# Attention, mixture of heads and a gated feed-forward on one core: four plain float32 pairs in batch 0 in place of two, under a new order table

## The chip, the cores and the metric

The kernel runs on one core of one Trainium2 chip. Its five engines run their own queues in order and wait for one another through semaphores: TensorE (PE) multiplies matrices into the eight PSUM banks, VectorE (DVE), ScalarE (ACT) and GpSimd (POOL) do elementwise work (POOL on SBUF alone in this kernel), and SyncE (SP) issues the transfers. The metric is the device time of one execution in microseconds (us); less is better.

## The reference

Three stages follow one another, all in float32, for 4 batches of 448 positions:

```python
# attention: q, k, v are [4, 12, 448, 64]
scores = scale * q @ k.T;  causal mask;  attn = softmax(scores);  x = attn @ v   # heads joined: [4, 448, 768]
# mixture: a gate picks 2 of 4 heads per position (weights from the gate's softmax over the two)
for e in range(4):
    a = softmax(causal(scale * (x @ wq[e]) @ (x @ wk[e]).T))
    out += gate[e] * (a @ (x @ wv[e]) @ wo[e])
# feed-forward: w_in is [768, 1024], a 3-tap convolution along the sequence gates the hidden values
h = relu(out @ w_in);  y = (h * sigmoid(conv3(h))) @ w_out
```

## The kernel before

A pair is two heads of one batch: `A0_3` is pair 3 of batch 0 of the attention (6 pairs a batch, 24 in all), `M1_0` a pair of the mixture (2 a batch). The second last number of a tile's name is the pair, a last `_1` or `_0` the head.

For each pair the steps are these. `prep` loads q and k. The *split form* loads each head onto both halves of the partitions (`nat`), copies it as float32r (the high part, line 333, 331 or 337) and subtracts to get the low part (line 340: one piece of 128x448 for k, one of 64x448 for q); on the stacked tile `sk` a head then needs two matmuls per row block (line 637). The *plain form* (`j.plain`) loads the pair once and `pair_scores` multiplies in plain float32 with 64 rows per head, both heads in turn for each row block (line 595); PE runs each such matmul as two records. The row blocks are 448, 336, 224 and 112 wide, since the mask is causal. DVE takes mask and row maximum out of PSUM into `P` (line 650), ACT the exponential (659), DVE the sum and reciprocal (667, 670), then POOL, ACT or DVE normalise the rows (333, 331, 337), PE transposes them against the identity (690, ten 112x112 blocks a head), ACT or DVE evacuate into `PT`, and PE multiplies with v in plain float32 (760, 16 records a pair, named PV here). Scores use the PSUM banks 0, 1 and 4 in turn (`s` in `BANKS`), transposes 2, 3 and 5, products 4 and 5.

Out of a batch's six `xT` tiles PE projects q, k (952) and v with the gate (998) of the mixture's heads, whose pairs then go the same way. The weights wo and w_in are folded into one matrix on the way (881, with conversions on DVE, ACT and POOL, lines 417 to 434, 869, 872), the feed-forward's first product is line 1188, its gate lines 1201 to 1226, and the output product line 1251 with 576 matmuls.

The order of all this isn't the program's: every step is a task, and a table (`ORDER`, decoded by `steps_of`) lists task numbers with the engine that runs each. `Program.run` goes through it, takes banks and buffers as the tasks ask for them, and issues each task's instructions there. So the table sets each engine's queue, and for steps that two or three engines can do, which of them does it. Where its own plan sees PE idle, it fills in matmuls of the identity (`warm`, line 1320), into a bank that `idle_bank` finds.

Of the kernel before, what the change touches and what calls it, by code (L numbers as in the profile page):

```python
# [1384 lines left out]
```

## Time and profile before

| | us |
|---|---|
| three runs | 500.73, 504.17, 504.58 (median 504.17) |
| profiled execution, its own time | 503.03 |
| its span, first to last instruction | 501.2 |
| PE busy in the span | 487.5 |
| DVE busy | 369.0 |
| ACT busy | 349.8 |
| POOL busy | 261.9 |

The span is what the trace shows of the execution; the 1.8 us around it are no instruction's. A busy PE counts the time in which a matmul is under way, and records of neighbouring matmuls overlap, so how much work PE has done is counted from the number of matmuls and the time that one takes in an unbroken stretch.

### The profile page before, as it was taken

How to read it: one execution, taken by the hardware profiler on the slowest of the kernel's cores; microseconds unless marked ns; L12 is line 12 of the kernel's file. 1: busy time of each engine (PE TensorE's matmuls, PEld its weight loads, DVE VectorE, ACT ScalarE, POOL GpSimd, SP SyncE). 2: the span in 40 equal slices, each digit the busy share in tenths (PEclk: the TensorE clock that was granted, in tenths of full speed). 3: DMA queues.
4: the chain of work that ended last, by engine and by line, in shares of the span. 5: the costliest groups of instructions: out<-in, count | busy, mean ns of one | idle time of the engine just before them, and what ended most of it. 6: DMA issues, size and time to landing. Idle time of an engine off the chain costs nothing.

```text
span 501.2 us, 9905 instructions
## 1 busy us (share of the span) xinstructions
PE 487.5 (97%) x3202; PEld 419.7 (84%) x3202; DVE 369.0 (74%) x1110; ACT 349.8 (70%) x970; POOL 261.9 (52%) x388
## 2 busy tenths in 40 slices
PE   8788999999999999999999999999999999999997
PEld 6656878988888898888988788898999989999996
DVE  4999999988899686987789984487587556374300
ACT  5989999998889768886888893386566554344201
POOL 1856879978879777998788944162022002000000
PEclk9999999999999999999999999999999999999999
DMA  8857468996793767665688615838220112101011
GB/s 216 211 164 186 128 179 225 232 250 192 203 242 106 178 173 214 142 176 136 202 204 237 151 57 168 272 148 213 88 90 0 56 37 80 51 16 58 37 38 73
DMA packets 29171, 73.03 MB, mean 146 GB/s; under 512 B 4160, under 2 KB 11072, under 8 KB 28352
## 3 DMA queue, kind: packets, MB, share of 16 engines
q1 hardware_dynamic: 29040, 72.18, 51.8%
q8 instruction: 25, 0.41, 0.4%
q10 hardware_dynamic: 80, 0.23, 0.2%
q14 instruction: 26, 0.21, 0.1%
HBM read 50.50 MB, written 13.63 MB: 128 GB/s over the span
## 4 chain that ended last, share of the span: by engine, by line
PE 74%; DVE 11%; POOL 5%; DMA 4%; issue 2%; ACT 1%; SPq 0%; POOLq 0%; DVEq 0%; ACTq 0%
PE bank L1251 23%; PE bank L952 9%; PE bank L690 9%; PE bank L760 9%; PE bank L637 9%; PE bank L1188 8%; PE bank L998 4%; DMA nat<-in_qk_dram 4%; DVE P_A L650 3%; PE bank L881 3%; POOL sk_A L340 2%; DVE PT_A L337 1%; POOL P_M L333 1%; POOL P_A L333 1%; DMA cwraw<-in_conv_w_dram 1%
## 5 line engine op out<-in xcount | busy, mean ns | idle before, releaser
L1251 PE MATMUL bank<-g,wout 128*128 128x448 f32 x576 | 123.2, 367 | 0.0
L1251 PEld LDWEIGHTS bank<-g,wout 128*128 128x128 f32 x576 | 107.4, 188 | 8.8
L659 ACT ACTIVATE P_A<-P_A,nm_A 112x448 f32<-112x448 f32 (+3 forms) x192 | 99.4, 521 | 15.7 <-DVE nm_A L650 10.4
L340 POOL TENSOR_TENSOR sk_A<-nat,sk_A 64x448 fp32r<-64x448 f32 (+1 forms) x77 | 90.3, 1172 | 9.7 <-ACT sk_A L331 3.9
L650 DVE CUSTOM_DVE_ANT_0 P_A<-bank,mask 112x448 f32<-112x448 f32 (+3 forms) x192 | 80.0, 440 | 10.8 <-PE bank L595 6.3
L637 PE MATMUL bank<-sk_A 128*112 128x112 f32 (+3 forms) x352 | 66.4, 312 | 3.5 <-DVE nm_A L650 2.9
L952 PE MATMUL bank<-xT,wqk 128*128 128x448 f32 x288 | 68.7, 374 | 0.6 <-DVE sk_M L968 0.4
L690 PE MATMUL bank<-ident,P_A 112*112 112x112 f32 x480 | 61.7, 264 | 3.3 <-DVE xT L792 1.4
L333 POOL TENSOR_SCALAR P_A<-P_A,r_A 112x336 f32<-112x336 f32 (+3 forms) x97 | 49.9, 526 | 25.7 <-DVE r_A L670 9.2
L637 PEld LDWEIGHTS bank<-sk_A 128*112 128x112 f32 x352 | 48.8, 176 | 10.1 <-DVE nm_A L650 4.5
L690 PEld LDWEIGHTS bank<-ident,P_A 112*112 112x112 f32 x480 | 49.8, 135 | 8.0 <-DVE xT L792 1.6
L952 PEld LDWEIGHTS bank<-xT,wqk 128*128 128x128 f32 x288 | 51.2, 188 | 4.1 <-DVE sk_M L968 0.5
L1209 DVE SCALAR_TENSOR_TENSOR bank<-h,cw,bank 128x448 f32<-128x448 f32 x64 | 43.5, 687 | 14.8 <-ACT bank L1207 11.6
L760 PE MATMUL bank<-PT_A,v 112*64 112x448 f32 (+3 forms) x384 | 50.4, 406 | 0.1
L760 PEld LDWEIGHTS bank<-PT_A,v 112*64 112x64 f32 x384 | 26.2, 137 | 23.6 <-issue 12.3
L331 ACT ACTIVATE P_A<-P_A,r_A 112x448 f32<-112x448 f32 (+3 forms) x87 | 42.3, 517 | 4.6 <-DVE r_A L670 4.3
L1188 PE MATMUL bank<-ocs,wp 128*128 128x448 f32 x192 | 43.5, 367 | 0.0
L998 PE MATMUL bank<-wvg,xT 128*112 128x260 f32 x288 | 41.2, 287 | 0.2 <-DVE wm L434 0.2
L333 POOL TENSOR_SCALAR sk_A<-nat 128x896 fp32r<-128x896 f32 x35 | 33.0, 941 | 12.6 <-DMA nat<-in_qk_dram 11.6
L1188 PEld LDWEIGHTS bank<-ocs,wp 128*128 128x128 f32 x192 | 35.7, 188 | 3.0
L659 ACT ACTIVATE P_M<-P_M,nm_M 112x224 f32<-112x224 f32 (+3 forms) x64 | 33.3, 522 | 6.8 <-DVE nm_M L650 5.3
L331 ACT ACTIVATE PT_A<-bank 112x336 f32<-112x336 f32 (+1 forms) x75 | 33.9, 472 | 5.2 <-PE bank L690 5.0
(105 smaller groups left out, 820.2 us busy)
## 6 DMA issues: line engine op xcount, KB each, us to landing
nat<-in_qk_dram SPq DMA_DIRECT2D x88, 224.0 KB, 4.0
wraw<-in_w_in_dram SPq DMA_DIRECT2D x12, 512.0 KB, 5.5
woraw<-in_w_out_dram SPq DMA_DIRECT2D x12, 512.0 KB, 5.1
wo<-wohl SPq DMA_DIRECT2D x12, 512.0 KB, 4.1
wout<-wo SPq DMA_DIRECT2D x6, 1024.0 KB, 10.0
v<-in_v_dram SPq DMA_DIRECT2D x24, 224.0 KB, 4.5
out_dram<-osb SPq DMA_DIRECT2D x24, 224.0 KB, 1.9
sk_M<-sk_M SPq DMA_DIRECT2D x16, 224.0 KB, 4.2
```

Of the source, the lines that this page charges most:

```text
L331: nc.scalar.activation(dst, src, AF.Copy, scale=scale)
L333: nc.gpsimd.tensor_scalar(dst, src, scale, 1.0 if scale2 is None else scale2, ALU.mult, ALU.mult)
L340: (nc.gpsimd if e == "POOL" else nc.vector).tensor_tensor(dst, a, b, op)
L637: nc.tensor.matmul(sp[:CP], t[:, j.o[h], m * CP : (m + 1) * CP], t[:, j.o[h] + k, :w], start=(k == 2), stop=(k == 1),)
L650: nc.vector.tensor_tensor_reduce(rows(i), st["s", i][:CP, :w], mask[:, S - w :], -SCALE, 3.0e38, ALU.add, ALU.min, st["nm"][:, i : i + 1],)
L659: nc.scalar.activation(rows(i), rows(i), AF.Exp, bias=st["nm"][:, i : i + 1], scale=-1.0, accum_out=st["sm"][:, i, 0:1],)
L690: nc.tensor.transpose(pt[:CP, o : o + CP], rows(i)[:, kt * CP : (kt + 1) * CP], ident[:CP, :CP])
L760: nc.tensor.matmul(st["ov"][h * D : (h + 1) * D, kt * CP : S], j.v[:, kt, h, :], j.PT[h][:, col_base[kt] : col_base[kt] + S - kt * CP], st ...
L952: nc.tensor.matmul(st["ps"][:, :S], proj["wqk"][:, a, cc, w, p * P : (p + 1) * P], xT[b, cc][:, b2, :], start=(cc == 0 and (a, b2) == PASS ...
L998: nc.tensor.matmul(st[i][:CP, :VW], xT[b, cc][:, a, i * CP : (i + 1) * CP], proj["wvg"][:, b2, cc, :], start=(cc == 0 and (a, b2) == PASSE ...
L1188: nc.tensor.matmul(st["ps", c][:, :S], wp[:, a, ec, c * P : (c + 1) * P], st["oc", ec][:, b2], start=(ec == 0 and (a, b2) == PASSES[0]), s ...
L1251: nc.tensor.matmul(st["ps"][:, :S], ffn["wout", n][:, a, c], gs[c][:, b2], start=(c == 0 and (a, b2) == PASSES[0]), stop=(c == NFC - 1 and ...
```

## The change

Pairs 2 and 3 of batch 0 take the plain form, as pairs 0 and 1 do already; their loads, scores and what feeds these change with it. The order table is another. A condition in `idle_bank` is added that holds for all eight banks.

```diff
-    "c-jrtxmQ{VqX2NYpm5n_6WQSc;$;!JfXb$<Dx0#(I)#`i#F;`(3N>FLW(qa)&WU8+IcTOZWC}G?s7aw_ieRQtGesm*sF^~|6fR#8%@i(Ey!TK1"
...
+    "c-jTQNj#eg!vOH)NkUdho+Pr0?6U7<Cwa0j$SRBPfX)H!fwTwoJ)m<yzk}!;&^d_C!SWu^9!TE<`X10Zh|U2s2eb!t4x)2F`~803|BpwqkS9nx"
...
                 o = self.owner.get(k)
-                if o is None or (o.left == 0 and o.ready <= since):
+                if k < 8 and (o is None or (o.left == 0 and o.ready <= since)):
                     return k
...
     for j in order:
-        j.plain = j.kind == "A" and j.b == 0 and j.p < 2
+        j.plain = j.kind == "A" and j.b == 0 and j.p < 4
```

What the table moves is seen in the queues themselves. Lines of the changed kernel are one lower (594 is 595 of before). On PE, just behind the plain scores of pair 1, this stood (`sk1_A0_2` is head 1 of pair 2 in split form, bank 2, 3 and 5 hold transposes):

```order
L637 MATMUL bank0_61<-sk1_A0_2_192 112x448 x2
L637 MATMUL bank4_65<-sk1_A0_2_192 112x224 x2
L637 MATMUL bank4_65<-sk1_A0_2_192 112x112 x2
L690 MATMUL bank2_63<-ident_71,P_A0_0_0_150 112x112 x4
L690 MATMUL bank3_64<-ident_71,P_A0_0_0_150 112x112 x3
L1320 MATMUL bank5_66<-ident_71 128x128 x2
L637 MATMUL bank1_62<-sk1_A0_2_192 112x336 x2
L690 MATMUL bank5_66<-ident_71,P_A0_0_0_150 112x112 x3
```

and this stands there now, with pair 2's plain scores of both heads on `sk0_A0_2`:

```order
L594 MATMUL bank1_62<-sk0_A0_2_217 112x448
L594 MATMUL bank4_65<-sk0_A0_2_217 112x448
L1319 MATMUL bank2_63<-ident_71 128x128 x2
L594 MATMUL bank0_61<-sk0_A0_2_217 112x336
L594 MATMUL bank1_62<-sk0_A0_2_217 112x336
L689 MATMUL bank2_63<-ident_71,P_A0_1_1_186 112x112 x4
L689 MATMUL bank3_64<-ident_71,P_A0_1_1_186 112x112 x3
L689 MATMUL bank5_66<-ident_71,P_A0_1_1_186 112x112 x3
L594 MATMUL bank0_61<-sk0_A0_2_217 112x224
L594 MATMUL bank1_62<-sk0_A0_2_217 112x224
```

The split scores of one head are replaced by plain ones of both heads, and the row blocks have transposes of pair 1 between them.

On POOL the queue began, behind the setting up of the masks, with the split parts of pairs 2 and 3 (`sk` from `nat`) and one normalisation of `P` a head:

```order
L333 TENSOR_SCALAR sk1_A0_2_192<-nat_0_2_1_193 128x2x448
L333 TENSOR_SCALAR P_A0_0_1_146<-P_A0_0_1_146,r_A0_0_1_148 112x336
L340 TENSOR_TENSOR sk1_A0_2_192<-nat_0_2_1_193,sk1_A0_2_192 128x448
L340 TENSOR_TENSOR sk1_A0_2_192<-nat_0_2_1_193,sk1_A0_2_192 64x448
L333 TENSOR_SCALAR P_A0_0_0_150<-P_A0_0_0_150,r_A0_0_0_152 112x336
L340 TENSOR_TENSOR sk1_A0_3_271<-nat_0_3_1_272,sk1_A0_3_271 128x448
L340 TENSOR_TENSOR sk1_A0_3_271<-nat_0_3_1_272,sk1_A0_3_271 64x448
L333 TENSOR_SCALAR P_A0_1_1_207<-P_A0_1_1_207,r_A0_1_1_209 112x448
```

and begins now with normalisations alone, up to the first split pair, which is pair 4:

```order
L332 TENSOR_SCALAR P_A0_0_1_146<-P_A0_0_1_146,r_A0_0_1_148 112x448
L332 TENSOR_SCALAR P_A0_0_1_146<-P_A0_0_1_146,r_A0_0_1_148 112x224
L332 TENSOR_SCALAR P_A0_0_0_150<-P_A0_0_0_150,r_A0_0_0_152 112x448
L332 TENSOR_SCALAR P_A0_0_0_150<-P_A0_0_0_150,r_A0_0_0_152 112x336
L332 TENSOR_SCALAR P_A0_0_0_150<-P_A0_0_0_150,r_A0_0_0_152 112x112
L332 TENSOR_SCALAR P_A0_0_0_150<-P_A0_0_0_150,r_A0_0_0_152 112x224
L332 TENSOR_SCALAR P_A0_1_1_186<-P_A0_1_1_186,r_A0_1_1_188 112x336
L332 TENSOR_SCALAR P_A0_1_1_186<-P_A0_1_1_186,r_A0_1_1_188 112x224
L332 TENSOR_SCALAR P_A0_1_0_190<-P_A0_1_0_190,r_A0_1_0_192 112x336
L332 TENSOR_SCALAR P_A0_1_0_190<-P_A0_1_0_190,r_A0_1_0_192 112x448
L332 TENSOR_SCALAR sk1_A0_4_335<-nat_0_4_1_336 128x2x448
L339 TENSOR_TENSOR sk1_A0_4_335<-nat_0_4_1_336,sk1_A0_4_335 128x448
```

Eight steps on `sk` before pair 1's last normalisation have gone, and POOL does two to four normalisations of a head where it did one.

On DVE, where the evacuations of pair 1 (`PT_A0_1`) are half done, this stood:

```order
L337 TENSOR_SCALAR PT_A0_1_1_1_339<-bank2_63 112x336
L337 TENSOR_SCALAR P_A0_1_0_211<-P_A0_1_0_211,r_A0_1_0_213 112x224
L340 TENSOR_TENSOR sk0_A0_3_386<-nat_0_3_0_387,sk0_A0_3_386 128x448
L650 ISA P_A0_2_0_377,nm_A0_2_0_378<-bank1_62,mask_76 112x336
L650 ISA nm_A0_2_0_378 112x1
L667 TENSOR_REDUCE r_A0_2_1_257<-sm0_88 112x4
L337 TENSOR_SCALAR PT_A0_1_1_0_340<-bank3_64 112x448
L670 RECIPROCAL r_A0_2_1_257<-r_A0_2_1_257 112x4
L650 ISA P_A0_2_0_377,nm_A0_2_0_378<-bank0_61,mask_76 112x112
```

and this stands there now (row maxima of pair 3 come in):

```order
L666 TENSOR_REDUCE r_A0_2_0_293<-sm1_90 112x4
L336 TENSOR_SCALAR PT_A0_1_1_0_309<-bank2_63 112x336
L649 ISA P_A0_3_1_391,nm_A0_3_1_392<-bank0_61,mask_76 112x448
L649 ISA nm_A0_3_1_392 112x1
L669 RECIPROCAL r_A0_2_0_293<-r_A0_2_0_293 112x4
L649 ISA P_A0_3_0_395,nm_A0_3_0_396<-bank4_65,mask_76 112x336
L649 ISA nm_A0_3_0_396 112x1
L649 ISA P_A0_3_1_391,nm_A0_3_1_392<-bank1_62,mask_76 112x336
```

The slow normalisation on line 337 and the low part on line 340 have left the stretch, and row maxima of the pair behind have moved up.

## Rows read from the trace of the kernel before

**Rows 1.** The page's first part: busy us (share) and instructions of each engine.

```profile
PE 487.5 (97%) x3202; PEld 419.7 (84%) x3202; DVE 369.0 (74%) x1110; ACT 349.8 (70%) x970; POOL 261.9 (52%) x388
```

**Rows 2.** Stretches: length, busy (x count) of PE, PEld, DVE, ACT, POOL, clock, DMA.

```profile
17.00:34.00 17.00, 13.37 (x91) 10.50 (x90) 16.62 (x52) 14.94 (x48) 11.97 (x13) 0.90 0.71 191
34.00:51.00 17.00, 14.79 (x110) 10.90 (x109) 16.90 (x51) 15.78 (x50) 9.58 (x11) 1.00 0.65 175
51.00:68.00 17.00, 16.57 (x121) 13.04 (x120) 16.79 (x60) 16.44 (x54) 15.42 (x20) 1.00 0.56 142
```

**Rows 3.** Waits of PE from 75 us on: us in total, times, longest.

```profile
PE bank L637 <- DVE nm_A L650: 0.4, 1, 0.4
...
PE bank L998 <- DVE wm L434: 0.2, 1, 0.2
```

**Rows 4.** PE's groups up to 73.6 us: count, busy us, mean ns, idle before.

```profile
L637 PE MATMUL bank<-sk_A 128*112 128x448 f32 (+3 forms) x97 | 18.8, 321 | 3.4 <-DVE nm_A L650 2.9 <-DVE xT L792 0.3
L690 PE MATMUL bank<-ident,P_A 112*112 112x112 f32 x130 | 17.6, 274 | 2.9 <-DVE xT L792 1.4 <-DVE P_A L337 0.7 <-DVE PT_A L337 0.4
L760 PE MATMUL bank<-PT_A,v 112*64 112x448 f32 (+3 forms) x96 | 13.0, 411 | 0.0
...
L952 PE MATMUL bank<-xT,wqk 128*128 128x448 f32 x30 | 7.8, 383 | 0.0
L595 PE MATMUL bank<-sk_A 64*112 64x448 f32 (+3 forms) x32 | 7.4, 444 | 0.7 <-DVE nm_A L650 0.7
```

**Rows 5.** The chain in order of time: start us, us, what.

```profile
68.31 1.23 PE bank L952 x6
69.54 1.11 PE bank L637 x8
70.65 0.96 PE bank L690 x10
71.61 2.04 PE bank L760 x16
...
461.70 35.88 PE bank L1251 x177
```

**Rows 6.** Plain scores: first block's stretch (length, PE, PEld); timeline's last (start, us).

```profile
5.49:6.52 1.03, 1.03 (x4) 0.36 (x4) 1.00 0.99 386
...
15.21 0.76 PE L595 MATMUL bank<-sk_A 64*112 64x112 f32 x4 [0.44 <-DVE nm_A L650]
```

**Rows 7.** Groups by shape over the span: count, busy us, mean ns, idle before.

```profile
L340 POOL TENSOR_TENSOR sk_A<-nat,sk_A 64x448 fp32r<-64x448 f32 x42 | 50.0, 1191 | 5.4 <-ACT sk_A L331 1.4 <-POOL P_A L333 0.8
L337 DVE TENSOR_SCALAR PT_A<-bank 112x336 f32<-112x336 f32 x44 | 21.5, 497 | 0.1
L331 ACT ACTIVATE PT_A<-bank 112x336 f32<-112x336 f32 x52 | 22.7, 443 | 3.9 <-PE bank L690 3.9
L331 ACT ACTIVATE P_A<-P_A,r_A 112x448 f32<-112x448 f32 x23 | 15.1, 661 | 1.9 <-DVE r_A L670 1.9
L331 ACT ACTIVATE sk_A<-nat 128x896 fp32r<-128x896 f32 x9 | 8.5, 948 | 0.5 <-DMA nat<-in_qk_dram 0.5
L340 DVE TENSOR_TENSOR sk_A<-nat,sk_A 128x448 fp32r<-128x448 f32 x9 | 7.7, 851 | 0.7 <-ACT sk_A L331 0.7
L337 DVE TENSOR_SCALAR P_A<-P_A,r_A 112x224 f32<-112x224 f32 x3 | 2.5, 833 | 0.0
L340 DVE TENSOR_TENSOR sk_A<-nat,sk_A 64x448 fp32r<-64x448 f32 x2 | 1.2, 622 | 0.1
```

**Rows 8.** Waits up to 75 us, longest first: us in total, times, longest.

```profile
POOL sk_A L333 <- DMA nat<-in_qk_dram: 11.0, 3, 9.8
```

**Rows 9.** PE's timeline from 20.93 us, and one stretch (columns as in rows 2).

```profile
20.93 0.57 PE L637 MATMUL bank<-sk_A 128*112 128x336 f32 x2 [1.95 <-DVE nm_A L650]
...
23.01 2.09 PE L690 MATMUL bank<-ident,P_A 112*112 112x112 f32 x10
...
20.00:30.00 10.00, 8.83 (x53) 6.55 (x53) 10.00 (x35) 9.59 (x32) 7.66 (x9) 0.83 0.66 174
```

More of the change, by code (lines that the diff above doesn't have):

```diff
@@ new lines @@
+    "t|LpxZRAkZ2I?Gji5jb#s5(HFktI|Gb%*MP!K-?!3RSaJROIi3L&9%pOclFISVgLmR)tV8RIzHgYOgAX>O%FS22k?qV0E<mgrKj^R(Dn3S6@}%"
+    "RO_pts$f;TDqHow>TQ*^8iO7|DX|8u4Qr|DtNuc`Bvc4cH50vE1w$WIT~ysxxv`@tK5P>8gYYW~Rx?mNT#cz2t)8qdRKKoXt$th0LzB=8)t6Np"
+    "=t0a7MuxtxDx;69j?p@_4edrJ&|!25J%%|)PhilnQuR)C1e?HiVt3IM^c}i@nZ+Dbm#e8YjGEKx^XdaM98<*P(B0@fb{IQ_<<~4>)-ji8G=_{B"
+    "#rC5I&|4TL#*E=%3Rs{TQ$2znLmy*iv3r<B>=t$zyNx}>tYIHv<+vP9ha*=H;<|AVE{IcL3>XL#$Mj(SjTTi;p_Mh-njbg>9)~C6A-tu=Qxm9("
+    ")dcbT*c`qa&%q1vGJF8Djk&<&YI<tQ*eI?SbBUQoXD~Ya9Qqb>j{&fG{4jnJFN1x?{)v6S%Ly)mj?jx6!kKYnxEt&x_6ZhA#Zk%B{+cKrjh)0j"
@@ new lines @@
+    "V6ixmz@)+nqxfmO7S@Yr;dnSRVF?!?fLI2WNtnaKaYg(#o`ib>8-|6bBh(l*LoHDG*fsoX+#B30+y-tJcZ55}^-%LQztLCeZ|Pg~Yx*8;6W>SO"
+    "#Enr|j0#=H7=um1&;%YKM#vHdV5@k5aezO?U*pg4ck~JBEEU5bF)na?MgdmAi>L~!foh`yGz^VJE92*D7Hjmhr-a9Z=Y&Uual#B?k+4#;QS)E="
+    "9=%K-pcbji)F915yTZ*8__Rqv1@|X?k+IB}g-ID})DP4p!XEXAal&xY-cygL7t|{%iDqWF7*bk^5oGKzt{72Tmex(P<2MLfgdM^yb)@EhMXyA!"
+    "MQ=n$B0zjhU1RJqZWz6cGsZmw&O8w@#Y40^>L0XY+IY=GO()|q?GYov$TP+n6AX;FP{U)sgKffw7(1|QQAKnonqkZ__F<)(-I~3ca?MlP3)&QI"
+    "p0+~!O#4b>)#_`@uuv_(HdfnR`v$fGv(%ErXQBn#8jZo6rcszUrkrVIhL|2|iS`5bZ_!)Pd(j8cl(;08)}Fx5U|(UkFrL_13xoI8exXxq|Dk=S"
@@ new lines @@
+    "A!;+VQKpWGfxDPwI1?@t^Wjps0X|qeT&oki#XGcu_*d_;cb~TIUGV0ZUChziXUrkyqSy)#h<C(W-evKQch8HfJ*vH~?PH$Qmc`dKw>1wn01=>L"
+    "iB5Q>HVFT#=8N|ircJyij*9ohv*PL6oVZ_{gm;Mt#3N#m$RIN574N+lL+2C6#Ft(k{jBz`_675k_a(E$yk_n&kC-P+xUa&L6ZOPn@wxa)jPbp!"
+    "eO+rMLPQc>Mt{v*tlg;n%ez&(TN@(oF-g9?+Bh*ogtL}vyNPd@tIRxWn5CnSvKCqW#5{3?h?9I5BP8F%phO_qVr{cxbha-*&%nFkeegl}FkC7b"
+    "Cr%NkSbE7B(=54T&JgE_w<I^+M$gf|)Ogs-tRQ<7{t~`I+#vSTOT=Abfpt$pvx-DAi^+<yJJ|=sBjP!cA-N)+5Z^I>g)hKGzBSe?tBbx2AEA%Z"
+    "4J-j!M&4(^$OH5h@+rAOo`J8!%d9Q<pDZcs8}W{)B_l{SmXKv3JIUwd9rzyn6I|)D__V$$y31Ff&(U!t3W-e;lJ3ZttlveDBp|_(Z&*LEd)ZIf"
@@ new lines @@
+    ">tu)(XZ5f$tTR?GE5O<%2YoS#jAS6id>P*<{DB2yW7#Y=iOpkE>z?_@WCnSkJmfnh+ej`_m=q(8`6hi+>=L`cF0+r>o8(1y!MDs_W6${(e3#@P"
+    "IYv&_J!e1i$=MJm&k1sN*ip_fr-#%}%9C;&cAc=UlhjFugOi+T&MbR`G){U%-eY6Hr{u@v5%Lsilru^ugWa5Swyds~GfkQ!U9n-DJN6WLp1eTL"
+    ")#dA^>WX#4b)$6!a-nXvZjrP?+8~ukyQBk>v97yr)i=kn148f%yvTXtyM*`FE!F+ZR)9LTg}q+4RcEVXgL)7G<KQ9bgcJbHpt}yo3D<$#Z)}kB"
+    "KazL8F3EPCfa3(D90upOE(`X6z2FDVTh10|m2<#3<eYLU@OwCu3kNU&2{`9K+$=Z9z2@9-^c)LE&J6-OZj}46?hEO$q>KBh?xOCt?!NA-?x}<g"
+    "!~lSc=JL2^ZXb7$`-=OVJIbBlj({_u02l)&z!h)@oCCAK0=N!tf_vb<BoCZ<?gF<P=mlO#CMB;VW$*<241NW_f#1QuNqWi(R|;4tAxeyrp{#Rz"
@@ L93 @@
+    "u0NO0P32~Cq0af-Vs0h3kt^kfb3f;HbNjhJa`DbwXHREu=d;fL2eqS|O#"
 )
```

104 lines of the change are left out of this document (41 added, 63 removed).

## The prediction

> **What bounds the kernel now.** I read the engine totals first, then stretches of the span, then who waited for whom, then the chain that ended last. TensorE (PE) is busy for 97% of the span, VectorE (DVE) for 74%, ScalarE (ACT) for 70%, GpSimd (POOL) for 52% [rows 1]. These are averages over two regimes, and the stretches tell them apart. From 17 to 68 us PE is busy for 44.7 of 51 us, while DVE is busy for 16.62 + 16.90 + 16.79 = 50.3 and ACT for 14.94 + 15.78 + 16.44 = 47.2 [rows 2]. After 75 us the waits put down to PE are five, of 0.4, 0.4, 0.3, 0.2 and 0.2 us, 1.5 us in all (first and last in [rows 3]). So there is a head of some 70 us in which softmax, evacuation and weight work on DVE and ACT feeds PE, and a body in which PE runs its queue without stopping. The chain says the same: from about 68 us it is PE nearly everywhere, and it ends with 35.88 us of output products in one piece [rows 5].
>
> What the head costs can be counted. When PE ends the weighted values of the last pair of batch 0 (A0_5), at 71.61 + 2.04 = 73.65 us [rows 5], it has done the work of [rows 4]: 96 score matmuls (12 heads; the row has one more that starts at the edge), 130 transposes, 96 records of PV, 30 projection matmuls and 2 plain pairs. At the rates of unbroken stretches [rows 5] that is 12 x 1.11 + 13 x 0.96 + 6 x 2.04 + 5 x 1.23, and 2 x 2.6 for the plain pairs (below): 13.3 + 12.5 + 12.2 + 6.2 + 5.2 = 49.4 us. PE has lost 24.3 us by then. That is what a change to batch 0 can win from.
>
> **The change part by part.** The sum is made against the profiled execution's own 503.0 us (span 501.2 us and 1.8 us around it). The median of the three runs is 504.2, so 1.1 above it, and one run was at 500.7.
>
> *PE work.* Pairs A0_2 and A0_3 lose four split heads, 4 x 1.11 = 4.4 us [rows 5], and get two plain pairs. The 448-wide row block of a plain pair, both heads, took 1.03 us in the first, undisturbed place [rows 6]; scaled by columns (1120 over 448) a pair is an estimate of 2.6 us, so two are 5.2. Below, the bound is no change: 40% of the columns of two split heads are worth 0.89 us at 1.11 a head, not far from 1.03. Above it is the busy time of the plain scores' records, waits between paired records included, 7.4 us for two pairs [rows 4], or +1.5 a pair. I take the estimate: **+0.8 us** (0 to +3.0).
>
> A plain score makes two PE records, which is 2 for a head's block where the split form also has 2 [rows 4, 6]. The Trainium skill, page "FP8 and Floating Point Precision", section "TensorE Precision Notes", says that true float32 takes four passes through the array. By that rule a plain pair would cost twice the split one, 2 x 2.2 us, so the sum would be 3.6 us higher, 504.2 us, still within 1% and for 0.04 of the chance of (c) below; the 1.03 us of the row speaks for a price near that of two.
>
> *PE order.* Up to the end of A0_5's products the new order holds 64 split score matmuls, 127 transposes, 24 projection matmuls, as many PV products and 4 plain pairs: 8.9 + 12.2 + 4.9 + 12.2 + 10.4 = 48.6 us. That is 0.8 less than the 49.4 above, and must be done later: **+0.8 us**.
>
> *DVE.* Up to the last evacuation before those products (PT_A0_5) the new order takes off DVE three normalisations of 112x224 (3 x 0.833), five evacuations of 336 (5 x 0.497) and one of 448 (0.6), three low parts 128x448 (3 x 0.851), and about 0.9 us of smaller things; it adds four low parts 64x448 (4 x 0.622) [rows 7]. That is 2.5 + 2.5 + 0.6 + 2.6 + 0.9 - 2.5 = 6.6 us of records; records on DVE overlap their successors by some 0.07 us and there are 11 fewer, so 5.8 us of time.
>
> *ACT.* To the same point: four normalisations of 448 fewer (4 x 0.661) and three smaller ones (about 0.4 each), two high parts fewer (2 x 0.948), one small exponential fewer (0.6), five evacuations of 336 more (5 x 0.443) and one of 448 (0.5), one weight copy more (0.6) [rows 7]: 2.6 + 1.2 + 1.9 + 0.6 - 2.2 - 0.5 - 0.6 = 3.0, with overlaps 2.7 us.
>
> *POOL* sheds eight low parts of 64x448 (8 x 1.191 = 9.5 us) [rows 7] and takes over ten normalisations, so its queue gets no longer while one of these takes under 0.95 us. It had room in the head (11.97 of 17 us from 17 to 34) [rows 2], so this is priced at nothing; the cover is that room, and were it gone, the normalisations that moved to POOL would make transposes late.
>
> *DMA and SP.* The plain loads carry each pair once where the split form carries it twice, 448 KB less a pair. POOL waited 9.8 us for the first split load [rows 8], but DVE had the row maxima of two pairs to do meanwhile, so nothing is counted. On SP the load of A0_1 moves ahead of the convolution weights, whose small steps on DVE and ACT come later; A0_2's load follows, and is needed only when two pairs' row maxima are read. The `k < 8` holds for every bank and changes nothing. After batch 0 the table changes banks and interleaving, with equal counts per kind on PE, so nothing is counted; the bounds are -1.5 us (the waits of [rows 3] gone) and +2 us (as much again and a little more).
>
> *How much of the relief reaches PE.* Between 17 and 68 us DVE idled 0.7 us and ACT 3.8 [rows 2]. Taking the relief off, each has about 44.5 us of work for what took 51. ACT alone would let the point come 2.7 us earlier with its idle time as it is; DVE, which was the full one, 5.8 us. Neither can hold the other at 99%, since each exponential waits for a row maximum and each evacuation for a transpose; I take **-4.0 us**, near the middle (2.7 to 5.8).
>
> Sum: 503.0 + 0.8 + 0.8 - 4.0 = **500.6 us**. Against -4.0 gained in the head stands 1.6 that PE pays back; the change breaks even when the point comes only 1.6 us earlier.
>
> **The rivals.**
> (a) *The whole relief and more* (faster). DVE sets the pace, all 5.8 us arrive, and since POOL and DVE stay ahead of PE afterwards the 1.5 us of later waits go too [rows 3]: 503.0 + 1.6 - 5.8 - 1.5 = 497.3 us, 1.1% faster. For it speaks that DVE was busy 98.6% from 17 to 68 us; against it, that ACT has only 2.7 us of relief.
> (b) *Plain scores in lockstep* (slower). In a plain pair every row block takes two banks at once out of three, so PE, which runs in order, waits for the row maxima of the block before, and the transposes behind it wait as well. In the kernel before PE waits at the plain scores for 0.7 us in all [rows 4], and the two pairs filled 5.49 to 15.97 us [rows 6], 10.5 us for 5.2 us of work. If two more pairs lose 2.6 us each and none of the relief arrives: 503.0 + 1.6 + 5.2 = 509.8, 1.3% slower. It decides as soon as the losses exceed the relief by 3.4 us. Against it: at the start there was nothing else to run, while in the new order transposes and PV products stand between the blocks.
> A piece of (b) is the clock. After PE had idled 1.95 us before 20.93 us, the granted clock of 20 to 30 us fell to 0.83, that is, part of it was spent at 1.2 of 2.4 GHz, and ten transposes took 2.09 us where 0.96 is usual [rows 5, 9]. One more such fall costs about 1.7 us (0.17 x 10). The Trainium skill, "TensorE: Matmul & The Clock Gate", section "A second HAM failure mode: psum-queue depth-cycling", tells of PE idling shortly as PSUM banks cycle and losing throughput to the changes of clock; the row shows one such fall, where PE waited for a bank that DVE had not read. By that rule a lockstep of the plain pairs would bring it again, 511.5 us with the above; one fall in a before-like head leaves it as it is.
> (c) *Relief off the path* (no change). The freed work was covered, ACT sets the pace with 2.7 us or less: 503.0 + 1.6 - 2.7 = 501.9, or, with 1.6, 503.0.
>
> **How the numbers follow.** About 1%, 5 us, is what a measurement of this kernel can tell from no change. Forecast (498.8 to 502, relief 2.7 to 5.8): 0.41. (c): 0.14. (a), with what else could make the later order better: 0.30. (b): 0.15. Forecast and (c) both lie within 1%: same 0.55, faster 0.30, slower 0.15. The likeliest one's own range is 498.5 to 503. The range that holds 8 in 10 reaches past (a) by the spread of single runs (500.7 to 504.6, so 2 us each way) to 495.5, and towards (b) up to 507.5.
>
> **What would show it.** Right: PE ends A0_5's products at about 69 to 70 us; the plain scores' waits for DVE stay below 2 us; DVE and ACT are both busy 94% or more from 17 to 64 us; counted PE work differs by about 1 us; the waits of PE after 75 us stay about 1.5 us. Wrong: a plain block of 448 that takes 1.5 us or more (the passes), a granted clock under 0.9 in more than one stretch of 10 us (lockstep), A0_5's products at 73 us or later (relief off the path), or a PE that waits 3 us or more after 75 us, which would be the new table and not the plain pairs.

## The result and the profile after

The changed kernel took **495.66 us** (median of four runs, 495.59 to 496.19), the kernel before 503.34 us beside it (four runs, 500.73 to 504.58). The ratio is 0.985, with a 95% interval of 0.981 to 0.989. A repetition (the run "The changed kernel again" below) gave 495.59 against 501.68 us, 0.986 (0.982 to 0.991). So it is faster by 1.2 to 1.5%. The predicted 500.6 us was too cautious: the time lies 0.16 us inside the low edge of the range (495.5 to 507.5), below the likeliest case's own 498.5 to 503, and past rival (a) with 497.3. Times are medians; two slow executions of one experiment below (509.13 and 596.54 us, the two pairs with DVE's waits for POOL charged) are left out of its median.

The profiled execution took 495.59 us, with a span of 493.8 us, against 503.03 and 501.2. The difference to explain is 7.4 us. Lines of the changed kernel carry numbers one lower than those of before.

The first part of its page, and the line of the chain by engine (PE had 74% of the chain before, now 88%):

```profile
PE 485.2 (98%) x3190; PEld 414.8 (84%) x3190; DVE 369.9 (75%) x1112; ACT 348.4 (71%) x966; POOL 246.8 (50%) x378
...
PE 88%; DVE 7%; ACT 3%; issue 1%; POOL 0%; DVEq 0%; POOLq 0%; ACTq 0%
```

The same stretches as in [rows 2], and the ten microseconds of [rows 9] (length, busy of PE, PEld, DVE, ACT, POOL, granted clock, DMA):

```profile
17.00:34.00 17.00, 16.73 (x106) 9.89 (x107) 16.90 (x64) 16.80 (x56) 12.05 (x17) 1.00 0.73 195
34.00:51.00 17.00, 15.45 (x118) 11.51 (x115) 16.82 (x58) 15.77 (x52) 10.57 (x13) 1.00 0.59 166
51.00:68.00 17.00, 16.90 (x127) 13.46 (x126) 15.84 (x59) 16.84 (x56) 15.03 (x20) 1.00 0.63 177
...
20.00:30.00 10.00, 9.89 (x64) 5.85 (x63) 9.96 (x38) 9.80 (x32) 5.93 (x9) 1.00 0.76 204
```

From 17 to 68 us PE is busy for 49.1 us (44.7 before), ACT for 49.4 (47.2) and DVE for 49.6 (50.3). Three engines now stand between 96 and 97%. The clock fall of 20 to 30 us (0.83) is gone.

PE's timeline where the third plain pair (A0_2) now stands, and the chain's piece with the products of A0_5, which [rows 5] has at 71.61 us:

```profile
16.94 1.01 PE L594 MATMUL bank<-sk_A 64*112 64x448 f32 x4
18.11 0.71 PE L1319 MATMUL bank<-ident 128*128 128x128 f32 x4 [0.16 <-DVE PT_A L336]
18.75 1.16 PE L594 MATMUL bank<-sk_A 64*112 64x336 f32 x4
19.84 1.31 PE L689 MATMUL bank<-ident,P_A 112*112 112x112 f32 x10
21.09 0.64 PE L594 MATMUL bank<-sk_A 64*112 64x224 f32 x4
21.65 2.11 PE L759 MATMUL bank<-PT_A,v 112*64 112x448 f32 x16
...
25.35 1.63 PE L594 MATMUL bank<-sk_A 64*112 64x448 f32 x4
```

```profile
64.33 2.04 PE bank L759 x16
```

Between the blocks of a plain pair stand transposes and products of A0_0, as the order promised. The products of A0_5 end at 66.37 us, 7.3 us earlier than 73.65. PE's groups up to that point (compare [rows 4]) and its waits after 75 us (compare [rows 3]):

```profile
L689 PE MATMUL bank<-ident,P_A 112*112 112x112 f32 x128 | 16.3, 265 | 0.0
L594 PE MATMUL bank<-sk_A 64*112 64x448 f32 (+3 forms) x64 | 14.8, 452 | 0.4 <-DVE nm_A L649 0.3
L759 PE MATMUL bank<-PT_A,v 112*64 112x448 f32 (+3 forms) x96 | 12.6, 406 | 0.0
L636 PE MATMUL bank<-sk_A 128*112 128x448 f32 (+3 forms) x64 | 12.5, 318 | 1.7 <-DVE nm_A L649 0.8 <-DVE sk_A L339 0.7
...
L951 PE MATMUL bank<-xT,wqk 128*128 128x448 f32 x24 | 5.9, 374 | 0.0
```

```profile
PE bank L997 <- DVE wm L433: 0.8, 1, 0.8
PE bank L1187 <- POOL ocs L1168: 0.4, 1, 0.4
PE bank L636 <- DVE nm_M L649: 0.2, 1, 0.2
```

**The account.** By the prediction's counts PE has done 49.4 us of work at that point before and 48.6 us after. It had lost 73.65 - 49.4 = 24.3 us and has now lost 66.37 - 48.6 = 17.8: **6.5 us less lost in the head**. From there to the end of the span are 427.55 us before and 427.43 us after, with 1.6 us more work left (0.8 from the order, 0.8 from the plain form as priced): **1.7 us less lost later**. 6.5 + 1.7 - 0.8 = 7.4. All of it lies ahead of the last product of the attention: from there (304.28 us before, 296.77 after) to the end it is 197.0 us in both. The profiled execution of before, in which the clock fell, took 503.03 us; against the medians beside the experiments (501.7 to 501.9) the gain is some 6.2 us and not 7.4.

Most of it is there early. PE ends the products of A0_0 at 27.98 us before (from 25.59 us, 2.39 long) and at 23.76 us after, and by the same rates has done the same work by then within 0.2 us. So some 4.2 of the 6.5 us are won in the first 28 us, where [rows 9] shows PE's wait of 1.95 us and the clock fall behind it.

That wait has a cause in the trace of before. The row maximum that PE waits for stands on DVE behind a low part of the gate weights (`wvg`), which takes 0.42 us elsewhere. It lasted 1.36 us here, about until POOL was through with two low parts of A0_3, which the change takes away (DVE's, POOL's and PE's timelines of before):

```profile
19.26 1.36 DVE L929 TENSOR_TENSOR wvg<-praw,wvg 128x260 fp32r<-128x260 f32 x1
...
17.65 2.69 POOL L340 TENSOR_TENSOR sk_A<-nat,sk_A 128x448 fp32r<-128x448 f32 x2 [0.58 <-ACT sk_A L331]
...
25.59 2.39 PE L760 MATMUL bank<-PT_A,v 112*64 112x448 f32 x16
```

So some 0.9 of the 1.95 us are DVE's standing still for POOL. In the changed kernel the same low part takes 0.41 us (at 19.67 us). What that is worth at the end is asked below.

### The profile page after: what moved, and what is told of

It is laid out like the page before. It is cut to its first block, busy times and chain, and to the rows that moved or that the text cites. A ratio compares the mean times of both kernels' runs of the same rounds, so it can differ in the third digit from the quotient of the medians.

```text
span 493.8 us, 9839 instructions
## 1 busy us (share of the span) xinstructions
PE 485.2 (98%) x3190; PEld 414.8 (84%) x3190; DVE 369.9 (75%) x1112; ACT 348.4 (71%) x966; POOL 246.8 (50%) x378
## 4 chain that ended last, share of the span: by engine, by line
PE 88%; DVE 7%; ACT 3%; issue 1%; POOL 0%; DVEq 0%; POOLq 0%; ACTq 0%
PE bank L1250 24%; PE bank L759 12%; PE bank L951 12%; PE bank L636 11%; PE bank L689 11%; PE bank L1187 8%; PE bank L997 6%; PE bank L880 3%; DVE P_A L649 2%; ACT P_A L658 2%; PE bank L594 1%; PE bank L1319 1%; DVE PT_A L336 1%; DVE sk_A L339 1%; DVE wvg L928 0%
## 5 line engine op out<-in xcount | busy, mean ns | idle before, releaser
L1250 PE MATMUL bank<-g,wout 128*128 128x448 f32 x576 | 121.6, 366 | 0.0
L339 POOL TENSOR_TENSOR sk_A<-nat,sk_A 64x448 fp32r<-64x448 f32 (+1 forms) x65 | 76.9, 1184 | 12.7 <-PE bank L951 3.8
L332 POOL TENSOR_SCALAR P_A<-P_A,r_A 112x448 f32<-112x448 f32 (+3 forms) x109 | 55.7, 524 | 38.6 <-DVE r_A L669 13.7
L636 PE MATMUL bank<-sk_A 128*112 128x448 f32 (+3 forms) x320 | 59.0, 310 | 1.9 <-DVE nm_A L649 0.8
L636 PEld LDWEIGHTS bank<-sk_A 128*112 128x112 f32 x320 | 44.5, 175 | 8.5 <-DVE nm_A L649 1.7
L332 POOL TENSOR_SCALAR P_M<-P_M,r_M,g_w 112x224 f32<-112x224 f32 (+3 forms) x56 | 32.9, 598 | 25.3 <-DVE r_M L669 23.7
L1197 POOL MEMSET h<- 128x2 f32 x32 | 3.1, 102 | 79.1 <-DVE bank L1218 66.0
L330 ACT ACTIVATE PT_A<-bank 112x336 f32<-112x336 f32 (+1 forms) x86 | 38.9, 471 | 1.0 <-PE bank L689 0.8
L658 ACT ACTIVATE P_M<-P_M,nm_M 112x112 f32<-112x112 f32 (+3 forms) x64 | 33.5, 525 | 7.4 <-DVE nm_M L649 7.4
L330 ACT ACTIVATE P_A<-P_A,r_A 112x224 f32<-112x224 f32 (+3 forms) x74 | 36.0, 508 | 3.9 <-DVE r_A L669 3.9
```

The source lines that it names most:

```text
L330: nc.scalar.activation(dst, src, AF.Copy, scale=scale)
L332: nc.gpsimd.tensor_scalar(dst, src, scale, 1.0 if scale2 is None else scale2, ALU.mult, ALU.mult)
L339: (nc.gpsimd if e == "POOL" else nc.vector).tensor_tensor(dst, a, b, op)
L636: nc.tensor.matmul(sp[:CP], t[:, j.o[h], m * CP : (m + 1) * CP], t[:, j.o[h] + k, :w], start=(k == 2), stop=(k == 1),)
L658: nc.scalar.activation(rows(i), rows(i), AF.Exp, bias=st["nm"][:, i : i + 1], scale=-1.0, accum_out=st["sm"][:, i, 0:1],)
L1250: nc.tensor.matmul(st["ps"][:, :S], ffn["wout", n][:, a, c], gs[c][:, b2], start=(c == 0 and (a, b2) == PASSES[0]), stop=(c == NFC - 1 and ...
```

## The experiments

Three questions were put: is it the plain form or the new order; does the lost clock count; and which engine's relief came through. In the expectations theory F is the form, O the order, L the lockstep of rival (b), C the clock, D and A are DVE and ACT as the pace, and P (in two meanings, told each time) is POOL.

### Form or order

**Four plain pairs in the order of before.** Against the changed kernel only the table differs:

```diff
 ORDER = (
...
-    "u0NO0P32~Cq0af-Vs0h3kt^kfb3f;HbNjhJa`DbwXHREu=d;fL2eqS|O#"
+    "noBLD7E>#!jZ`tUm-6>T`u0<Qq*8tTeFJ?z_5Cm1GMq{"
 )
```

> Four plain pairs put into the order of the kernel before: each instruction that both kernels have keeps its place and its engine as far as the buffers allow, the plain scores of A0_2 and A0_3 stand where the scores of their first heads stood, and the low and high parts are gone. Theory F (the plain form is worth the gain by itself, whatever the order): the 7.3 us that A0_5's products came earlier show up here too, 495 to 499 us. Theory L (the form pays only with its blocks spread out, since a block holds two of three banks until DVE has read both): PE waits for row maxima at the plain scores for several us more than the 0.3 us of the changed kernel, and the time is at or above that of before, 503 to 512 us. Theory O (the order is what was won): no gain either, 501 to 505 us, without those waits.

Measured: **513.99 us** against 501.92, ratio 1.024 (1.021 to 1.027). PE's timeline in the scores of A0_3, and the group of throwaway products (they fill the gaps that the planner foresees; 9.4 us of them stand up to 85 us in the kernel before):

```profile
30.87 1.01 PE L589 MATMUL bank<-sk_A 64*112 64x448 f32 x4
31.81 3.39 PE L1314 MATMUL bank<-ident 128*128 128x128 f32 x28
35.13 1.08 PE L589 MATMUL bank<-sk_A 64*112 64x336 f32 x4
36.14 1.16 PE L1314 MATMUL bank<-ident 128*128 128x128 f32 x8
37.23 0.64 PE L589 MATMUL bank<-sk_A 64*112 64x224 f32 x4
37.80 4.96 PE L1314 MATMUL bank<-ident 128*128 128x128 f32 x42
```

```profile
L1314 PE MATMUL bank<-ident 128*128 128x128 f32 x166 | 24.0, 299 | 1.4 <-POOL ident masks.py:199 1.4
```

Theory L holds, at a price above its 512 us. One sign of it is not there: PE hardly shows as waiting at the plain scores (0.5 us), since 24.0 us of throwaway products stand where it would wait. Each of these blocks of A0_3 is followed by one to five microseconds in which PE has nothing of its own. At A0_2, whose blocks have transposes and products between them in this table too, nothing is lost: PE ends the products of A0_0 at 26.05 us (27.98 before). It ends those of A0_1, which come behind the blocks of A0_3, at 45.53 us (36.86 before). Nor is any engine full meanwhile: from 34 to 51 us DVE is busy for 9.77 of 17 us and ACT for 10.73. By the timelines they wait for one another: DVE's queue, as in the order of before, has the second head's row maximum far behind the first's (DVE's timeline, the 336-wide maxima of A0_3):

```profile
35.98 0.51 DVE L644 CUSTOM_DVE_ANT_0 P_A<-bank,mask 112x336 f32<-112x336 f32 x1 [0.64 <-PE bank L589]
...
49.48 0.50 DVE L644 CUSTOM_DVE_ANT_0 P_A<-bank,mask 112x336 f32<-112x336 f32 x1
```

So in this order, which neither puts other work between the blocks of A0_3 nor reads their banks soon, the plain form loses 2.4%. Which of the two costs how much was not tested.

**Two plain pairs in another order.**

```diff
 ORDER = (
...
-        j.plain = j.kind == "A" and j.b == 0 and j.p < 4
+        j.plain = j.kind == "A" and j.b == 0 and j.p < 2
```

> Two plain pairs as in the kernel before, but the order of the first 900 steps and the engines of the free steps searched anew (about one in four changes its place). Theory O (a new order is what was won, the form hardly counts): 495 to 499 us, A0_5's products end at 66 to 69 us. Theory F or L (the four plain pairs take the load off the head): no more than the scatter of before, 500.5 to 504.5 us, products at 71 to 74 us.

Measured: **503.77 us** against 501.92, ratio 1.004 (1.002 to 1.006). PE ended A0_5's products at 70.2 us, a little earlier than I gave theory F, and the time did not follow: PE lost it again in the mixture, above all in one wait of 1.8 us. A new order for two pairs wins nothing.

**Four plain pairs in another order.** Again only the table differs from the changed kernel:

```diff
 ORDER = (
...
-    "u0NO0P32~Cq0af-Vs0h3kt^kfb3f;HbNjhJa`DbwXHREu=d;fL2eqS|O#"
+    "mapVT^3U?y`Q7{<`9xQ~tGBDK>v7lr1N(8DLI"
 )
```

> Four plain pairs as in the changed kernel, the order of the first 900 steps searched anew from its table. If what counts is the load that four plain pairs take off, with any order that spreads them: 494.5 to 497 us, products of A0_5 at 65.5 to 67.5 us. If the one table of the changed kernel was lucky: 498 to 503 us.

Measured: **499.33 us** against 501.92, ratio 0.996 (0.993 to 0.999). That is 4.4 us below the two pairs searched in the same way, but 3.7 above the changed kernel, between the two expectations. The products of A0_5 end at 66.0 us, with 2.4 us less work done ahead of them than in the changed kernel, so the point alone would mislead here. PE's two largest waits up to 75 us, behind the 1.4 us at the very start, are ones the changed kernel does not have at that length:

```profile
PE bank L589 <- DVE nm_A L644: 1.5, 2, 1.3
PE bank L684 <- DVE PT_A L331: 1.4, 1, 1.4
```

**The changed kernel again**, as the base of the runs below.

> The changed kernel itself, as the base of the three runs beside it and beside the other order of four plain pairs (499.3 us). All theories: 495 to 497 us.

Measured: **495.59 us** against 501.68.

### The clock

**The kernel before, kept busy in its gap.** Against the kernel before:

```diff
-                    fill(int((start - end[e] - 200) / (260 if end[e] else 430)), end[e])
+                    fill(int((start - end[e] - 200) / (260 if end[e] else 430)) + (6 if n == 239 else 0), end[e])
```

> The kernel before with six more throwaway products of the identity where PE waited 1.95 us for DVE at 20.93 us, nothing else. Theory C (the fall of the granted clock behind that wait is part of what the change won back): the granted clock from 20 to 30 us is 1.00 in place of 0.83, the time falls by 1 to 2 us to 500.7 to 502 us, and its runs scatter by less than the 3.9 us of before. Rival (PE has other waits behind it that take up the loss): the clock stays up, the time is that of before within 0.5 us.

Measured: **502.27 us** against 501.92, ratio 1.001 (0.999 to 1.003). Its runs scatter as much as those of before (499.5 to 504.1 us). The clock stayed up as expected in the profiled execution (PE's timeline, then the stretch):

```profile
19.00 2.05 PE L1320 MATMUL bank<-ident 128*128 128x128 f32 x16
20.81 0.55 PE L637 MATMUL bank<-sk_A 128*112 128x336 f32 x2
```

```profile
20.00:30.00 10.00, 8.26 (x66) 6.42 (x65) 10.00 (x35) 10.00 (x34) 8.34 (x9) 1.00 0.67 179
```

The products of A0_0 ended 2.0 us earlier than before, those of A0_5 0.9 us, and at the end nothing was left: the rival is right. In the head of before, DVE and ACT are full, so what PE gains at one place it waits for at the next. The kernel before itself says what a fall goes with: in 82 of its runs beside these experiments, the 46 with a mean clock of 0.998 or more took 501.1 us on average, the 30 at 0.995 to 0.997 took 502.8 and the 6 below 504.1. That is 1.7 us between the first two groups, but a late DVE that makes PE wait longer would bring both the fall and the time, so it is not shown that the fall costs it. The eight runs of the changed kernel have 0.998 or more.

### Which engine's relief

**A dose on each engine.** Into the changed kernel, behind the first row maximum (or exponential) of the heads of A0_1 to A0_5, went work whose result nobody reads:

```diff
+            if n in EXTRA:
+                extra()
...
+    def extra():
+        nc.vector.tensor_tensor(spare, mask[:, :336], mask[:, :336], ALU.subtract)
```

on DVE; on ACT and on POOL it was

```diff
+        for _ in range(2):
+            nc.scalar.activation(spare, mask[:, :336], AF.Copy)
...
+        nc.gpsimd.tensor_tensor(spare[:64], mask[:64, :336], mask[:64, :336], ALU.subtract)
```

> The changed kernel with nine subtractions of 112x336 more on DVE, into a tile that nobody reads, one behind the first row maximum of a head from A0_1 to A0_5: an estimate of 0.65 us each from the 0.851 us of 128x448, 5.9 us in all. Theory D (DVE sets the pace of the head, so relief on DVE reaches the end nearly whole): 499.5 to 502 us, 4 us or more above the changed kernel. Rival A (ACT sets the pace, or PE itself does in the changed kernel, DVE has room): under 2 us above, up to 497.7 us.

> The changed kernel with fourteen copies of 112x336 more on ACT, two behind the first exponential of seven heads from A0_2 to A0_5, into a tile that nobody reads: 0.44 us each by the evacuations of that width, 6.2 us in all. Theory A (ACT, busy 49.4 of 51 us from 17 to 68 us, now sets the pace as much as DVE): 4 us or more above the changed kernel, 499.7 us or later. Theory D (only DVE sets it): under 2 us above, up to 497.7 us.

> The changed kernel with seven subtractions of 64x336 more on POOL, one behind the first row maximum of seven heads, into a tile that nobody reads: an estimate of 0.9 us each from the 1.191 us of 64x448, 6.3 us in all. By the working of the prediction POOL has room in the head (12.05 of 17 us busy from 17 to 34 us in the changed kernel), so its relief was priced at nothing: within 1 us of the changed kernel. Rival P (the 9.5 us of low parts that POOL sheds were a part of the gain): 2 us or more above, 498 us or later.

The doses as the traces show them (count, busy us, mean ns), of DVE, ACT and POOL:

```profile
L1328 DVE TENSOR_TENSOR spare<-mask 112x336 f32<-112x336 f32 x9 | 7.7, 857 | 0.0
```

```profile
L1329 ACT ACTIVATE spare<-mask 112x336 f32<-112x336 f32 x14 | 6.7, 478 | 0.2
```

```profile
L1328 POOL TENSOR_TENSOR spare<-mask 64x336 f32<-64x336 f32 x7 | 6.4, 908 | 0.2
```

Measured: DVE **499.15 us** (+3.6, of a dose of 7.7), ACT **499.88** (+4.3 of 6.7), POOL **501.38** (+5.8 of 6.4). DVE stays short of the 4 us of theory D and well over the 2 of its rival; ACT meets theory A. Both set the pace in the head, and about half to two thirds of what is put on either comes out at the end. (The DVE doses took 0.50 to 1.35 us each in the profiled execution, the slowest of its ten, so their 7.7 us hold some standing still of the kind below.) The third was the surprise: POOL, busy 12.05 of 17 us, costs nearly as much as was put on it. Its place of damage (POOL's, DVE's and PE's timelines of that run, then a stretch):

```profile
18.49 1.89 POOL L1328 TENSOR_TENSOR spare<-mask 64x336 f32<-64x336 f32 x2
20.36 1.15 POOL L337 TENSOR_SCALAR P_A<-P_A,r_A 112x336 f32<-112x336 f32 x2
21.49 0.93 POOL L337 TENSOR_SCALAR sk_A<-nat 128x896 fp32r<-128x896 f32 x1
...
19.70 3.00 DVE L934 TENSOR_TENSOR wvg<-praw,wvg 128x260 fp32r<-128x260 f32 x1
...
23.18 1.51 PE L600 MATMUL bank<-sk_A 64*112 64x224 f32 x4 [2.19 <-DVE nm_A L655]
24.62 4.00 PE L765 MATMUL bank<-PT_A,v 112*64 112x448 f32 x16
...
20.00:30.00 10.00, 7.81 (x39) 4.45 (x38) 7.68 (x20) 5.61 (x17) 4.74 (x6) 0.66 0.56 157
```

A low part of the gate weights on DVE, which takes 0.42 us alone, lasts 3.00 us, about until POOL pauses at 22.42. The row maximum behind it is late, and PE waits 2.19 us at a plain block whose bank nobody has read. Behind that the granted clock of 20 to 30 us is 0.66, and the 16 products of A0_0 take 4.00 us where they took 2.11. They end at 28.62 us, 5.4 later than in the changed kernel profiled beside it (23.25); the whole span is 6.6 longer. So most of the cost arises at this one place, behind the first two of seven doses, and is no rate at which POOL's work is passed on. Every run of this kernel had a mean granted clock of 0.992 to 0.997; how much of the 5.8 us the fall is was not tested apart. DVE and ACT are not full there (7.68 and 5.61 of 10 us), unlike in the test of the clock above.

**The same dose, writing only.** The seven subtractions became fourteen fills:

```diff
-        nc.gpsimd.tensor_tensor(spare[:64], mask[:64, :336], mask[:64, :336], ALU.subtract)
+        for _ in range(2):
+            nc.gpsimd.memset(spare, 0.0)
```

> The changed kernel with fourteen fills of 112x336 more on POOL, two in the place of each of the seven subtractions of the dose before that cost 5.8 us: an estimate of 0.36 us each from the 0.472 us of the fill of 112x448, 5.0 us in all, and POOL reads nothing in them. In the run with the subtractions one DVE subtraction of 128x260 (0.42 us alone) took 3.00 us while POOL ran four instructions without a break, and DVE records were 5.8 us longer than usual up to 75 us, against 1.7 to 2.8 in the changed kernel. Theory P (what cost the time is that DVE instructions with two operands in SBUF stand still while POOL reads there): the subtractions of 128x260 keep 0.4 to 1.4 us, the time is within 1.5 us of the changed kernel, 495 to 497 us. Rival Q (POOL's own queue was late, and normalisations and low parts behind it): the same cost as with the subtractions, 499.5 to 502 us.

Here "theory P" is that POOL's reading of SBUF stops DVE. The dose, and the low parts on DVE (shortest, median and longest ns):

```profile
L1329 POOL MEMSET spare<- 112x336 f32 x14 | 5.3, 379 | 0.6
```

```profile
L934 DVE TENSOR_TENSOR wvg<-praw,wvg x4: 416/420/1361, 19.0 to 34.8; 128x260 fp32r<-128x260 f32 x4
```

Measured: **497.28 us**, 1.7 above the changed kernel, with 5.3 us of dose against 6.4 and a cost of 1.7 against 5.8. (This run and the repetition of the changed kernel were on two chips, on which the kernel before took 501.82 and 501.68 us.) Theory P had said 1.5 at most and the rival 4 or more, so most of the cost came of DVE being stopped. With the fills the products of A0_0 end as early as in the changed kernel (23.20 us), so what they cost comes later; that it is POOL's own queue is likely and not shown. The Trainium skill, "SBUF — State Buffer", section "Who interferes with whom", says that a DVE instruction with two SBUF inputs contends with a GpSimd instruction that reads SBUF, not with one that only writes; the two doses agree (longest low part 3.00 us with the reading dose, 1.36 with the fills, beside which POOL's other work still reads).

**Was that what the change won?** By the change the low parts of A0_2 and A0_3 go, eight in all, seven of them on POOL. This run takes them out of the kernel before and leaves its order:

```diff
+    def bare(j):
+        return j.kind == "A" and j.b == 0 and j.p in (2, 3)
...
+            if bare(j):
+                return lambda e: None
             return lambda e: two(e, j.sk[h][:, 1, :], st["nat"][:, 1], f(j.sk[h][:, 2, :]), ALU.subtract)
...
-                            t[:, j.o[h] + k, :w],
+                            t[:, j.o[h] + (2 if bare(j) else k), :w],
```

> The kernel before without the eight low parts of A0_2 and A0_3 (seven on POOL, some 8.3 us, one on DVE, 0.85 us); the second product of their scores reads the high part again, so that PE does the same work on other numbers. Order, engines and everything else stay. By the working of the prediction (POOL's relief is worth nothing): 0 to 1 us less than before, 501 to 502 us. Theory P (POOL's reading stops DVE, so what POOL sheds is a relief of DVE): DVE records are stretched by less than the 7.1 us of before up to 75 us, and the time falls by 2 to 5 us, 497 to 500 us.

Measured: **504.23 us** against 501.82, ratio 1.003 (1.000 to 1.007). In the profiled execution, which at 500.74 us was the fastest of ten, POOL is relieved (6.44 us busy of 17, 11.97 before), DVE and ACT are as full as ever and PE is hardly busier (14.17 against 13.37):

```profile
17.00:34.00 17.00, 14.17 (x96) 9.97 (x96) 16.53 (x60) 16.58 (x56) 6.44 (x8) 0.93 0.75 193
```

At the place of the 1.95 us it did what theory P says (PE's timeline, with the products of A0_0):

```profile
18.90 0.56 PE L644 MATMUL bank<-sk_A 128*112 128x336 f32 x2 [0.79 <-DVE nm_A L657]
22.49 2.11 PE L767 MATMUL bank<-PT_A,v 112*64 112x448 f32 x16
```

The low part of the gate weights took 0.42 us, PE waited 0.79 us, the granted clock of 20 to 30 us stayed at 1.00, and the products of A0_0 ended at 24.60 us, 3.4 earlier than before. Those of A0_1 then took 3.70 us behind a wait of 1.74, those of A0_5 ended only 1.4 us earlier, and the median gained nothing. So POOL's load can cost much where it stops DVE, yet taking it away in the order of before gave nothing at the end. Theory P falls as an account of the whole change. It does account for much of the early gain, which this order loses again.

**Orders that keep DVE clear of POOL.** Tables for two and for four pairs, searched like those above, with DVE's waits for POOL charged. The two-pair one again has `j.p < 2`; the other has only another table:

```diff
 ORDER = (
...
-    "u0NO0P32~Cq0af-Vs0h3kt^kfb3f;HbNjhJa`DbwXHREu=d;fL2eqS|O#"
+    "U&)W=f6njZ_ws+_6W#glzV80+C*A)KQfHh?"
 )
```

> Two plain pairs, as in the kernel before, in an order searched anew with the planner's costs, but with the port counted as the traces show it: a DVE instruction on SBUF data waits until POOL pauses, and not the other way round. Theory P (what the changed kernel won is DVE's time free of POOL, by whatever means): PE ends A0_5's products by 67 us, and the time is that of the changed kernel or less, 490 to 497 us, with no pair more in plain float32. Theory F (the plain form is needed): 500 to 504 us.

> Four plain pairs as in the changed kernel, in an order searched in the same way with the port counted. Theory P: faster than the changed kernel (495.6 us) by 2 to 6 us, 490 to 493.5 us, and within 2 us of the two pairs searched in this way. Theory F: 494.5 to 496.5 us, and 5 us or more below the two pairs.

Measured: two pairs **504.60 us** against 501.82, ratio 1.005 (1.001 to 1.008); four pairs **498.41 us**, ratio 0.994 (0.991 to 0.996). Theory F is right for the two pairs. For the four pairs neither figure holds: 2.8 us slower than the changed kernel, 6.2 faster than the two pairs. Its trace shows a place where it is no better: PE waits at plain blocks, and the clock falls behind that (PE's timeline, then the stretches):

```profile
30.80 0.87 PE L589 MATMUL bank<-sk_A 64*112 64x224 f32 x4 [1.40 <-DVE nm_A L644]
...
35.28 2.09 PE L684 MATMUL bank<-ident,P_A 112*112 112x112 f32 x10
37.30 2.74 PE L754 MATMUL bank<-PT_A,v 112*64 112x448 f32 x16
```

```profile
17.00:34.00 17.00, 14.85 (x88) 9.04 (x85) 16.33 (x56) 15.01 (x51) 12.64 (x17) 0.93 0.63 167
34.00:51.00 17.00, 16.80 (x111) 12.78 (x110) 14.18 (x55) 14.80 (x45) 9.26 (x11) 0.86 0.72 193
```

The expectation has it that DVE waits for POOL and not the other way round, and the searches charged it so; the traces have both. In the changed kernel a normalisation of 112x448 on POOL (0.64 us elsewhere) took 1.33 us at 19.18 us, while DVE ran two low parts of weights.

Put side by side:

| order | two pairs | four pairs | four less two |
|---|---|---|---|
| the tables of before and of the change | 501.7 to 501.9 | 495.59 | -6.1 |
| searched with the planner's costs | 503.77 | 499.33 | -4.4 |
| searched with DVE's waits for POOL charged | 504.60 | 498.41 | -6.2 |
| order of before kept | 501.92 | 513.99 | +12.1 |

In each of the three kinds of spread-out order four pairs beat two, by 5.6 us on average, and each four-pair order beats each two-pair one. Within one column these orders differ by up to 2.8 us (two pairs) and 3.7 us (four). None of these kernels beats the changed one.

## Why the prediction was right or wrong

- **What bounds the kernel: right.** A head that DVE and ACT feed, and a body that PE fills. The doses confirm the head: DVE and ACT both pass on about half or more. That the time fell inside the range is luck: its lower end had been moved 2 us past rival (a) for the scatter of single runs, and the time sits on that end, 4.9 us below the sum.
- **PE work, +0.8 us: not contradicted.** The undisturbed 448-wide block took 1.01 us where I had taken 1.03. The longer blocks, 1.34 and 1.63 us, hold waits between paired records, which was one of my marks for "wrong"; the mark was badly chosen, since it could not tell passes from waits. By the Trainium skill ("FP8 and Floating Point Precision", "TensorE Precision Notes") plain float32 takes four passes; the time that I derived from that, a pair at twice the split price, is not what the 1.01 us shows.
- **PE order, +0.8 us: right.** The counts ahead of A0_5's products are those of the trace: 64 split and 64 plain records, 128 transposes (127 forecast), 24 projections.
- **Relief, -4.0 us: the step that failed, by its size.** The point came 7.3 us earlier, beyond my upper bound of 5.8. I had written that neither engine could hold the other at 99% and taken the middle of 2.7 and 5.8. In place of that DVE kept its pace (49.6 us busy of 51) and ACT rose from 47.2 to 49.4. And some 4.2 us were gone by A0_0's products, at a place that I had read and set aside: [rows 9] shows PE idle for 1.95 us and a clock of 0.83 behind it, and I treated one such fall as a property of any such head. In the new order the plain blocks of A0_2 stand there with work between them, and neither the wait nor the fall occurs. Nothing in the sum stood for that. The fall alone does not account for it, as the run kept busy shows. Some 0.9 us of the wait were DVE held by POOL, as the trace of before shows, and without POOL's low parts A0_0's products came 3.4 us earlier in a trace with the order of before. That order did not keep the gain; that the new one does because PE has other work between the blocks is read from the two timelines and was not tested alone.
- **The order as a term of its own: missing, and the form too low.** Two other orders of the same four pairs take 498.4 and 499.3 us, 2.8 and 3.7 more than the changed kernel, and the sum had no term for that. But the table of before is better than two other orders of two pairs as well, by 1.9 and 2.8 us, so about 1 us of the 6 is left for the new table's being the better one of its kind. Against two pairs searched in the same way, four pairs win 4.4 and 6.2 us, where the sum (503.0 to 500.6) gave the change 2.4. So it is mostly the form in a spread-out order that I priced too low, not the table that I left out. Three pairs of tables are few, and why one table is better is shown only so far: the other four-pair ones have waits of 1.3 and 1.4 us at scores and transposes which it has not.
- **POOL priced at nothing: for a wrong reason, and not settled.** The room in POOL's time was no cover: 6.4 us of reading put there cost 5.8, most of it at one place. Taking the low parts away was worth nothing at the end in the order of before. In the new order, where the early gain is kept, their going may be worth something; no run took the change without it.
- **Later, 0 us (-1.5 to +2): 1.7 us less was lost, just outside.** PE's waits there stayed 1.4 us (1.5 expected), so it is not they. It comes ahead of the attention's last product, and its cause stays open.
- **Rival (a)** was nearest, with its 5.8 us, but its other half (the waits of 1.5 us gone) did not happen. **Rival (b)** was real: 513.99 us in the order of before, even over my 509.8. I was right that transposes and products between the blocks prevent it. Its clock piece showed in the last four-pair order and with the dose on POOL. **Rival (c)** is out.
- **The marks.** A0_5 at 69 to 70 us: no, 66.4. Plain scores waiting for DVE under 2 us: yes, 0.3. DVE and ACT above 94% busy: yes (98 and 97% from 17 to 64 us). Clock below 0.9 in more than one stretch: none. Waits of PE after 75 us of 3 us or more: no, 1.4.

## What to carry to other kernels

A form that takes two banks at once is worth what the order makes of it: the same four plain pairs gave -6 us, -3 us or +12 us against the kernel before, so price the form and its place together, and test it in more than one order. A long wait of the bound engine that stands in the profile of before belongs in the sum, as a term that goes or stays, not in a rival. And an engine with idle time is no cover by that alone: put a dose on it, see what comes out, and find the place where it arises before taking it for a rate. Compare an order with others only where both sides have had the same search.

## What the runs showed of the hardware that was not expected

POOL reading SBUF held a DVE subtraction of two SBUF tiles for 3.00 us in place of 0.42, not for one POOL instruction but over several, until POOL paused. A dose of 6.4 us of such reading on POOL cost 5.8 us, one of 5.3 us of fills 1.7. It goes by who is first: counted over the records of all fourteen traces, DVE's low parts of q, k and weights that began with no POOL instruction under way were never held (0 of 210 by more than 0.1 us), of those that began under a POOL subtraction of `sk` 58 of 83 were, under a normalisation of `P` 10 of 36, under a fill 0 of 4. The other way round, 117 of 140 POOL normalisations, copies and subtractions that began under such a low part were held. DVE's busy time counts this standing still: the mean of 0.833 us for a normalisation of 112x224 in [rows 7], on which a term of the sum rested, was for the most part waiting, as the same instruction took 0.33 us in the run with four pairs in the order of before (at 27.38 us).
